# Moving three loads and one weight sum within a fused pooling-attention and MLP kernel

## The chip, the cores and the metric

The kernel runs on one core of a Trainium2 chip. The metric is device time in microseconds from the first to the last instruction of one execution, given as the median of several runs. The engines are TensorE (PE, matmuls; PEld is its weight load), VectorE (DVE), ScalarE (ACT), GpSimd (POOL) and SyncE (SP), which issues most of the data transfers.

## The reference

For each of 8 batches and 8 heads there are 576 positions of width 64. Keys and values are averaged over runs of 8 positions, so that 72 of each are left; queries are not pooled. Attention over the 72 pooled keys is followed by a two-layer perceptron on the joined heads (width 512, hidden width 2048, tanh form of Gelu):

```python
k_p = k.reshape(B, H, 72, 8, D).mean(axis=3)
v_p = v.reshape(B, H, 72, 8, D).mean(axis=3)
attn = softmax(q @ k_p.T / sqrt(D))          # per batch and head
x = (attn @ v_p) laid out as (B*S, 512)      # 4608 rows
out = gelu_tanh(x @ w_in) @ w_out            # (4608, 512), float32
```

## The kernel before

**Groups and steps.** The 4608 rows are worked in nine groups of 512: group b holds positions 0 to 511 of batch b, and one more group (`R`) collects the last 64 positions of all eight batches. `seq` is their order: 0 to 6, R, 7. One step of the program is the perceptron of one group, with the attention of the next group and the loads of the one after that placed between its matmuls. So in step 1 the matmuls are those of group 1, the attention is that of group 2 (`n`), and the loads are for group 3 (`n2`).

**What sets the order.** There is no scheduler: the order on each engine is the order in which the code emits instructions. `at(hooks, s, f, ...)` puts a call at position s of the step. Positions 0 to 63 are the matmuls of the first layer (the hidden half; one per matmul of 512 columns, four matmuls for one of 16 blocks of the hidden layer), and 64 to 175 are those of the second layer (the output half), seven products of 16 matmuls each. Both layers of the later steps use a seven-product scheme in place of eight products, which needs sums of operand blocks: `w_sums` makes four sums of blocks of `w_out` (once, into `tw`), `g_sums` sums of the hidden activations (each step), `x_sums` sums of the inputs. Step 1 uses the plain first layer (`hidden_two`, `hidden`, L554 and L397) and the seven-product second layer; from step 2 on `hidden_fast` does the first layer with seven products too, partly (L500).

**Attention of the next group.** Pooling is three adds on DVE: L162 (8 to 4), L164 (4 to 2), L165 (2 to 1, into `kvb`). For K, `dup_k` (L178) writes a second copy, a DMA transpose (L225, `kTd`) turns it, and GpSimd spreads it into `kbd` (L94). Queries are cast to bf16 (`q_b`, L94 or L92) and turned by a DMA transpose (L246, `qT`). V goes through GpSimd's masked spread (L185, `vbd`). The scores (L262) go to `e` by an exponential on ACT (L271), DVE makes the row sums (`den`, L278) and the reciprocal `r` (L287), POOL or DVE normalises into `eb` (L293), four DMA transposes (L320) give `eT`, and the weighted sums (L358) give `xT`, the next group's input.

**Loads.** K and V of a group lie in the tiles `k_sb` and `v_sb`, each with one buffer; `k_sb` holds 512 of the 576 pooled rows of K in four chunks, and its fifth chunk is half K and half V. So `load_kv` has a K part of three transfers (`k_sb`: 1 MB, 128 KB, 128 KB; part 0) and a V part of one (`v_sb`, 1 MB; part 1). A part can go out only when the pooling of the group before has read the buffer. Queries (`q_sb`, 1 MB, two buffers) are loaded by `load_q` on SP, or by `load_q_behind` on POOL: a one-column copy into `gate` that reads the tile named, and so waits for its landing, and then the transfer from POOL's queue.

**What the change touches.** In step 1 (`n_ == 1`, L861 to L865 and L917 to L939): the place of the third sum of `w_out` blocks, L862; the place and queue of group 3's queries, L919 and L926 to L930; the place of group 3's K part, L938. In step 2 (`n_ == 2`): the first pooling add of group 3's K, L895. In the hidden half of a fast step (L518 to L543), DVE's instructions L525, L533, L536 and L540 free or finish the PSUM banks that PE's products share, and the K pooling stands between them at the position that L895 gives.

Of the kernel before, what the change touches and what calls it, by code (L numbers as in the profile page):

```python
# [19 lines left out]
def kernel(  # L20
# [21 lines left out]
    nc = tc.nc  # L42
    B, H, S, D = q.shape
# [44 lines left out]
    st = [dict() for _ in range(B + 1)]  # L88
# [711 lines left out]
    def at(hooks, s, f, *a):  # L800
        hooks.setdefault(s, []).append(lambda: f(*a))
# [6 lines left out]
    hooks = {}  # L808
# [47 lines left out]
    for n_, g in enumerate(seq):  # L856
        if n_ == 0:
            continue
        hooks = {}
        fast = n_ >= 2  # L860
        if n_ == 1:  # L861
            for i, s in enumerate((1, 10, 14)):  # L862
                at(hooks, s, w_sums, 1 + i, 0, NP, nc.vector)
            at(hooks, 36, g_sums, 0, 4)
            at(hooks, 57, g_sums, 4, 6, (0,))  # L865
        else:
            at(hooks, 41, g_sums, 0, 2, (0,))
            at(hooks, 57, g_sums, 2, 6, (0,))
            at(hooks, 65, g_sums, 6, 8, (0,))
            at(hooks, 65, g_sums, 0, 4, (1,))  # L870
        if not fast:
            at(hooks, 65, g_sums, 6, 8, (0,))
        at(hooks, 64 + 32, g_sums, 4, 8, (1,))
        if n_ == 6:
            at(hooks, 30, late_stores)
        if n_ + 1 < len(seq):
            n = seq[n_ + 1]
            b = B - 1 if n == R else n
            kv = n != B - 1
            if n_ == 1:  # L880
                at(hooks, 18, cast_q, n, 0, 1, nc.scalar)
                at(hooks, 18, cast_q, n, 2, 4, nc.gpsimd)
                at(hooks, 22, cast_q, n, 1, 2, nc.scalar)
                at(hooks, 24, qT_tile, n)
                at(hooks, 24, q_transpose_dma, n)
            if kv and not fast:
                at(hooks, 2, pool, b, 0, 5)
                at(hooks, 2, dup_k, b, 0, 5)
                at(hooks, 2, kT_tile, b, None)
                at(hooks, 2, k_transpose_dma, b)  # L890
                at(hooks, 24, pool, b, 5, 9)
                at(hooks, 26, k_spread, b, [nc.gpsimd, nc.gpsimd])
                at(hooks, 26, spread_v, b, nc.gpsimd)
            elif kv:
                at(hooks, 5, pool, b, 0, 5, (0,))  # L895
                at(hooks, 17, pool, b, 0, 5, (1,))
                at(hooks, 17, dup_k, b, 0, 5)
                at(hooks, 17, kT_tile, b, None)
                at(hooks, 17, k_transpose_dma, b)
                at(hooks, 17, spread_gated, b)  # L900
                at(hooks, 40, k_spread, b, [nc.gpsimd, nc.gpsimd])
            sc_at = [68, 68, 90, 90]
            for j in range(4):
                at(hooks, sc_at[j], scores, n, j)
                at(hooks, sc_at[j] + 1, exps, n, j)
            at(hooks, 80, eT_tile, n)
            for j in range(4):
                at(hooks, 80 if j < 2 else 92, norm, n, j, nc.vector if j > 1 and fast else nc.gpsimd)
                at(hooks, 80 if j < 2 else 92, e_transpose_dma, n, j)
            at(hooks, 64 + 66, nc.scalar.preload_act_table_set, GELU_SET)  # L910
            at(hooks, 64 + 100, xT_tile, n)
            if n_ == 1:
                at(hooks, 64 + 100, values, n, (0,))
                at(hooks, 64 + 107, values, n, (1,))
            else:
                at(hooks, 64 + 104, values, n)
        if n_ + 2 < len(seq):  # L917
            n2 = seq[n_ + 2]
            s2 = 1 if n_ == 1 else 30  # L919
            for half, ahead in enumerate((3, 2)):  # L920
                if n_ + ahead < len(seq) and seq[n_ + ahead] == R:
                    if half == 0:
                        at(hooks, 2, q_tile, R)
                    at(hooks, 2, load_q_behind, R, st[g]["xT"][64:128, KO - 1, MAIN - 1:MAIN], 2 * half, 2 * half + 2)
            if n2 != R:
                at(hooks, s2, q_tile, n2)  # L926
                if n_ == 1:
                    at(hooks, s2, load_q_behind, n2, st[n]["k"][64:128, 4, 7, D - 1:D], 0, 4)
                else:
                    at(hooks, s2, load_q, n2, 0, 4, nc.sync)  # L930
            at(hooks, 64 + 52, cast_gated, n2)
            at(hooks, 64 + 94, qT_tile, n2)
            at(hooks, 64 + 94, q_transpose_dma, n2)
            if n2 != B - 1:
                b2 = B - 1 if n2 == R else n2
                at(hooks, 64 + 84, pool, b2, 5, 9, (0,))
                at(hooks, 64 + 97, pool, b2, 5, 9, (1,))
            at(hooks, 29 if n_ == 1 else 28, load_kv, n2, (0,))  # L938
            at(hooks, 28 if n_ == 1 else 1, load_kv, n2, (1,))  # L939
        mlp(g, hooks, n_ + 1 == len(seq), fast)  # L940

# [29 lines left out]
```

The softmax here doesn't subtract the row's maximum and nothing guards it: scores larger than these inputs give would overflow.

## Time and profile before

| | |
|---|---|
| Time, median of 3 runs | 281.07 us (278.54 to 282.31) |
| Profiled execution | 278.88 us, span 277.2 us |
| PE busy | 269.3 us, 97% of the span |
| DVE / ACT / POOL busy | 226.2 / 176.4 / 86.7 us |
| Data moved | 54.37 MB, mean 196 GB/s |
| Step 1 | about 51.5 to 81.8 us |
| Step 2 | about 81.8 to 109.4 us |

In the profile a group's line names the code line, the engine, the operation, and the output and input tiles; a wait line reads "engine, its line, what it waited for: us in total, times, longest". In the chain and the timelines the first column is the start in us from the start of the span and the second the duration in us. "DMA to landing" is the time from issue of a transfer to its completion.

### The profile page before, as it was taken

The numbers are of one execution on the slowest core, as the hardware profiler recorded it, in microseconds if no ns is written. First come the engines' busy times: TensorE is split into PE (matmuls) and PEld (weight loads), VectorE is DVE, ScalarE is ACT, GpSimd is POOL, SyncE is SP. The second block draws the span as 40 slices with busy tenths as digits, with TensorE's granted clock in tenths as the row PEclk, the third lists the DMA queues.
The fourth block names the chain that finished last, engine by engine and source line by source line (L and its number), as shares of the span: only waits on it lengthen the run. The fifth ranks groups of instructions, "written<-read, shape, count | busy, mean of one in ns | idle before, by whom it ended". The sixth has DMA issues, their size and how long they took to land.

```text
span 277.2 us, 6633 instructions
## 1 busy us (share of the span) xinstructions
PE 269.3 (97%) x2710; PEld 195.5 (71%) x2710; DVE 226.2 (82%) x368; ACT 176.4 (64%) x261; POOL 86.7 (31%) x129
## 2 busy tenths in 40 slices
PE   8989999999999999999999999999999999999995
PEld 3778844445876688668766886688668866886684
DVE  5896869899889899989898999899989458956832
ACT  1576576568546965696469656965696469656820
POOL 4640282045843142224453345233224200300000
PEclk9999999999999999999999999999999999999999
DMA  7999999999989958894999789928393920243013
GB/s 228 310 189 293 368 386 222 281 363 196 266 148 313 283 132 192 257 290 109 193 265 263 193 187 296 234 53 180 118 286 75 173 98 0 50 102 99 2 40 114
DMA packets 67088, 54.37 MB, mean 196 GB/s; under 512 B 41458, under 2 KB 52722, under 8 KB 67058
## 3 DMA queue, kind: packets, MB, share of 16 engines
q1 hardware_dynamic: 64146, 49.62, 68.5%
q0 software_dynamic: 2768, 4.20, 7.7%
q8 instruction: 21, 0.34, 0.5%
q10 hardware_dynamic: 144, 0.13, 0.1%
q14 instruction: 9, 0.07, 0.1%
HBM read 36.70 MB, written 9.44 MB: 166 GB/s over the span
## 4 chain that ended last, share of the span: by engine, by line
PE 65%; DMA 10%; DVE 7%; issue 1%; ACT 1%; POOL 1%; SPq 1%; DVEq 0%; ACTq 0%; POOLq 0%
PE mm L609 28%; PE mm L397 16%; PE c L500 14%; DMA eT<-eb 5%; PE x L609 3%; DMA qT<-q_b 2%; PE xo L358 2%; DMA k_sb<-in_v_dram 2%; PE sc L262 2%; DVE den L278 1%; DVE eb L293 1%; DVE k_sb L162 1%; DVE k_sb L164 1%; DVE kvb L178 0%; ACT e L271 0%
## 5 line engine op out<-in xcount | busy, mean ns | idle before, releaser
L397 PE MATMUL mm<-xT,w_in_b 128*128 128x512 bf16 x280 | 65.5, 379 | 0.4 <-ACT gT L399 0.4
L609 PEld LDWEIGHTS <-gT 128*128 128x128 bf16 x512 | 48.3, 98 | 9.0 <-issue 1.4
L399 ACT ACTIVATE gT<-mm 128x512 bf16<-128x512 f32 x70 | 39.7, 598 | 16.0 <-PE mm L397 15.9
L397 PEld LDWEIGHTS <-w_in_b 128*128 128x128 bf16 x280 | 27.4, 98 | 27.8 <-issue 0.9
L609 PEld LDWEIGHTS <-stage 128*128 128x128 bf16 x384 | 37.6, 98 | 4.3
L293 POOL TENSOR_TENSOR eb<-e,r 128x576 bf16<-128x576 f32 x16 | 18.5, 1179 | 49.2 <-DVE r L287 26.8
L92 ACT CAST xT<-xo 128x512 bf16<-128x512 f32 (+1 forms) x24 | 13.2, 610 | 28.4 <-PE xo L358 24.1
L609 PE MATMUL mm<-tw,gT 128*128 128x256 bf16 x240 | 30.0, 273 | 0.0
L609 PE MATMUL mm<-w_out_b,gT 128*128 128x256 bf16 x240 | 29.9, 273 | 0.0
L271 ACT ACTIVATE e<-sc 128x576 f32<-128x576 f32 x36 | 22.3, 649 | 9.7 <-POOL eb L293 5.4
L278 DVE TENSOR_REDUCE den<-e 128x8 f32<-128x576 f32 x36 | 26.3, 731 | 2.5 <-ACT e L271 2.5
L500 PEld LDWEIGHTS <-ws 128*128 128x128 bf16 x224 | 21.9, 98 | 7.0
L609 PE MATMUL mm<-tw,stage 128*128 128x256 bf16 x224 | 26.7, 273 | 0.0
L92 ACT COPY osb<-mm 128x512 f32<-128x512 f32 x29 | 17.2, 592 | 13.7 <-PE mm L609 13.6
L185 POOL TENSOR_TENSOR vbd<-kvb,vmask 128x256 bf16<-128x256 bf16 (+2 forms) x38 | 21.6, 590 | 5.8 <-DVE kvb L165 4.7
L94 POOL CAST q_b<-q_sb 128x1024 bf16<-128x1024 f32 (+1 forms) x16 | 17.1, 1087 | 19.4 <-DMA q_sb<-in_q_dram 19.4
L500 PE MATMUL c<-tt,ws 128*128 128x256 bf16 x168 | 20.6, 273 | 0.0
L500 PEld LDWEIGHTS <-w_in_b 128*128 128x128 bf16 x168 | 16.4, 98 | 2.4 <-issue 0.2
L408 PE MATMUL mm<-xT,w_in_b 128*128 128x256 bf16 x128 | 15.6, 273 | 0.1
L293 DVE TENSOR_TENSOR eb<-e,r 128x576 bf16<-128x576 f32 x16 | 15.0, 940 | 0.6
L609 PE MATMUL mm<-w_out_b,stage 128*128 128x256 bf16 x128 | 15.3, 273 | 0.0
L459 DVE TENSOR_TENSOR gT<-gT 128x512 bf16<-128x512 bf16 (+1 forms) x24 | 12.9, 536 | 2.4 <-ACT gT L516 0.5
(118 smaller groups left out, 439.1 us busy)
## 6 DMA issues: line engine op xcount, KB each, us to landing
q_sb<-in_q_dram SPq DMA_DIRECT2D x6, 1024.0 KB, 8.8
k_sb<-in_k_dram SPq DMA_DIRECT2D x6, 1024.0 KB, 7.7
v_sb<-in_v_dram SPq DMA_DIRECT2D x6, 1024.0 KB, 8.2
out_dram<-osb SPq DMA_DIRECT2D x12, 512.0 KB, 4.1
w_in_b<-in_moe_w_in_dram POOLq DMA_DIRECT2D x4, 512.0 KB, 6.7
w_out_s<-in_moe_w_out_dram SPq DMA_DIRECT2D x2, 1024.0 KB, 13.9
stage<-in_moe_w_out_dram SPq DMA_DIRECT2D x2, 1024.0 KB, 15.3
out_dram<-osb SPq DMA_DIRECT2D x7, 256.0 KB, 2.8
```

What stands on the lines that cost most here:

```text
L92: eng.copy(out=out, in_=in_)
L94: eng.tensor_copy(out=out, in_=in_)
L185: eng.tensor_tensor(out=vbd[p0:128, b, n0:n1, :].rearrange("p (c r) (hh d) -> p c (r hh) d", c=max(m, 1), d=D), in0=kvb[p0:128, 4 + c0:4 + ...
L271: nc.scalar.activation(out=e.rearrange("p (x h) s -> p x (h s)", x=2), in_=sc[:, :, 0:4 * Sp], func=ACT.Exp, scale=1.0 / 64.0)
L278: nc.vector.reduce_sum(out=den, in_=e, axis=AX.X)
L293: eng.tensor_tensor(out=o.rearrange("p (pr hh s) -> p hh pr s", hh=2, s=Sp), in0=e.rearrange("p (hh pr) s -> p hh pr s", hh=2), in1=r.rear ...
L397: nc.tensor.matmul(out=hp, lhsT=w_in_b[:, ko, fo * 128:(fo + 1) * 128], rhs=st[g]["xT"][:, ko, :], start=(i == 0), stop=(i == KO - 1))
L399: nc.scalar.activation(out=gT[:, fo, :], in_=hp, func=ACT.Gelu_apprx_tanh)
L408: nc.tensor.matmul(out=hp[:, f, :], lhsT=w_in_b[:, ko, (fo + f) * 128:(fo + f + 1) * 128], rhs=st[g]["xT"][:, ko, c0:c0 + 256], start=(i = ...
L459: nc.vector.tensor_tensor(out=a21, in0=a21, in1=a22, op=ALU.add)
L500: nc.tensor.matmul(out=acc[:, m, :], lhsT=lhs(i, m), rhs=rhs(i), start=bool(fresh and i == 0 and m % 2 == 0), stop=(i == 1), skip_group_ch ...
L609: nc.tensor.matmul(out=xs[p] if acc is xs else acc[:, p, :], lhsT=lt, rhs=rt, start=bool(fresh and m == 0 and (p == 0 or (last and acc is ...
```

## The change

Four edits. The third of step 1's `w_sums` moves from hook 14 to hook 97, right behind the sum of `g_sums` that the sixth product reads; what it makes (`tw[3]`) is first read by the seventh product, from hook 160. Group 3's queries go out on SP at hook 29, behind its V part at hook 28, and not on POOL behind the landing of group 2's K tile. Group 3's K part goes from hook 29 to hook 93, which is behind the last two DMA transposes of group 2's softmax weights (hook 92). As K comes later, its first pooling add in step 2 moves from hook 5 to hook 11. The purpose is to keep the loads of group 3 out of the way of group 2's transfers and transposes, and to take the weight sum out of DVE's way ahead of the softmax.

```diff
         if n_ == 1:
-            for i, s in enumerate((1, 10, 14)):
+            for i, s in enumerate((1, 10, 64 + 33)):
                 at(hooks, s, w_sums, 1 + i, 0, NP, nc.vector)
...
             elif kv:
-                at(hooks, 5, pool, b, 0, 5, (0,))
+                at(hooks, 11 if n_ == 2 else 5, pool, b, 0, 5, (0,))
                 at(hooks, 17, pool, b, 0, 5, (1,))
...
-            s2 = 1 if n_ == 1 else 30
+            s2 = 29 if n_ == 1 else 30
...
             if n2 != R:
                 at(hooks, s2, q_tile, n2)
-                if n_ == 1:
-                    at(hooks, s2, load_q_behind, n2, st[n]["k"][64:128, 4, 7, D - 1:D], 0, 4)
-                else:
-                    at(hooks, s2, load_q, n2, 0, 4, nc.sync)
+                at(hooks, s2, load_q, n2, 0, 4, nc.sync)
...
-            at(hooks, 29 if n_ == 1 else 28, load_kv, n2, (0,))
+            at(hooks, 93 if n_ == 1 else 28, load_kv, n2, (0,))
             at(hooks, 28 if n_ == 1 else 1, load_kv, n2, (1,))
```

## The prediction, made before the result was known

> **What bounds the kernel now.** I read the page first, then busy time by stretch, the waits of the tensor engine alone, the chain, and the vector engine's timeline around the edit.
>
> ```profile
> PE 269.3 (97%) x2710; PEld 195.5 (71%) x2710; DVE 226.2 (82%) x368; ACT 176.4 (64%) x261; POOL 86.7 (31%) x129
> ```
>
> PE is the bound: 269.3 of 277.2 us. All that any edit of order can give back is PE's idle time, 7.9 us in the whole span. The stretches show where it lies around the edit (step 1's hidden half, its output half, step 2's hidden half, its output half; after the stretch come length, then busy us of PE, PEld, DVE, ACT, POOL, then clock, DMA share, GB/s):
>
> ```profile
> 53.00:66.00 13.00, 12.60 (x59) 5.57 (x58) 11.44 (x14) 9.29 (x17) 3.92 (x4) 1.00 1.12 289
> 66.00:82.00 16.00, 15.22 (x212) 12.17 (x211) 13.79 (x24) 8.98 (x14) 12.09 (x13) 1.00 1.01 216
> 82.00:95.00 13.00, 13.00 (x90) 8.61 (x88) 11.82 (x18) 10.21 (x15) 3.63 (x8) 1.00 1.04 295
> 95.00:109.00 14.00, 14.00 (x206) 11.72 (x205) 13.24 (x23) 8.05 (x12) 4.80 (x5) 1.00 0.68 153
> ```
>
> Step 1 idles PE 0.40 + 0.78 us; step 2 not at all. So the edit can win at most about 1.2 us where it works, and step 2, which it also touches, can only lose. The waits of PE from 53 to 82 us, and the chain there, name the idle time:
>
> ```profile
> PE sc L262 <- DMA qT<-q_b: 0.6, 1, 0.6
> PE mm L397 <- ACT gT L399: 0.4, 1, 0.4
> ```
>
> ```profile
> 60.39 6.78 DMA qT<-q_b
> 67.17 0.04 issue
> 67.21 0.46 PE sc L262 x32
> ...
> 73.88 4.86 DMA eT<-eb
> 78.75 0.14 issue
> 78.88 0.75 PE xo L358 x16
> ```
>
> The scores of group 2 wait 0.64 us for the query transpose, which takes 6.78 us from issue to landing, where the one of group 3 took 4.4 at 79.60. The weighted sum waits 0.14 us for the second transpose of softmax weights: 4.86 us, where such transposes took 2.6 us in quiet stretches. Both transposes run beside loads of group 3: its queries (GpSimd's queue, issued 56.40, 7.1 us to landing) and its V and K (SyncE's, from 65.12). The 0.40 us is ScalarE: its casts wait for group 2's queries, landed at 57.76, and a Gelu stands behind them.
>
> The vector engine, start and duration:
>
> ```profile
> 60.03 1.21 DVE L451 TENSOR_TENSOR tw<-w_out_b,tw 128x2048 bf16<-128x2048 bf16 x1
> ...
> 70.34 0.74 DVE L278 TENSOR_REDUCE den<-e 128x8 f32<-128x576 f32 x1
> ...
> 82.67 1.49 DVE L162 TENSOR_TENSOR k_sb<-k_sb 128x1280 f32<-128x1280 f32 x1
> 84.07 1.22 DVE L525 TENSOR_TENSOR other<-c,other 128x1024 f32<-128x1024 f32 x1
> ...
> 87.43 1.21 DVE L533 COPY stage<-c 128x1024 f32<-128x1024 f32 x1
> 88.89 1.23 DVE L536 TENSOR_TENSOR stage<-c,stage 128x1024 f32<-128x1024 f32 x1 [0.26 <-PE c L500]
> ```
>
> The first weights became ready at 68.68 (ScalarE's exponentials start at 68.08) but were reduced only at 70.34: DVE was late there by 1.66 us. In step 2 the first half of K's pooling (L162) fills a hole before L525, and everything up to L536 is back to back.
>
> **What the Trainium skill says.** "DMA: Bandwidth & Descriptors", section "Issuing engines are not separate DMA queues": DMAs from GpSimd and SyncE end on the same 16 engines and interleave. The trace agrees: the transposes were slowest (6.4 and 6.8 us) while the GpSimd queue's 1 MB was in flight. The same page, "Measured (HBM→SBUF, 128 partitions, SWDGE, issued from GpSimd)", gives 6.15 us for 1 MB alone; this trace has 5.7 to 10.3 us for the pieces of a K load, and I use those. "SBUF — State Buffer", section "Who interferes with whom": a VectorE instruction with two SBUF inputs and a GpSimd one that reads SBUF lock each other out. The trace agrees: L462 took 0.80 us at 65.72, 1.07 us at 74.29 beside GpSimd's normalisation, one of which took 1.60 us instead of 1.15.
>
> **The change part by part.**
>
> *Third weight sum (1.21 us) from hook 14 to hook 97.* On DVE it leaves 60.03 and comes after the fourth operand sum (L462), at about 74.4. Everything between moves up by at most 1.2 us. The pooling of V(2) right behind it needs V(2)'s landing, 49.55 + 10.8 = 60.35, so I take 1.0. den starts at 69.3, GpSimd's four normalisations (71.44 to 76.37) end near 75.4, and the last weights' transpose, issued at 77.2 now, goes at about 75.5. Behind the sum stand L623 and L594; L594 reads x before the last product may add to it. Now L594 ends at 77.36, 0.78 us before that product (78.14). Then it ends at 77.36 - 1.0 + 1.2 = 77.6 if the sum costs its plain 1.2, and the product is due at 78.14 - 0.64 = 77.5: a stall of 0.1 us, up to 0.5 if the port lock stretches the sum to 1.6. With DVE's 0.70 us idle before L594 to absorb a part, I take 0. V(3)'s pooling and the xT cast behind have 0.69 us of idle time now: 0.
>
> *Queries of group 3 to SyncE at hook 29.* The load leaves GpSimd (a 1.50 us gate and a 0.96 us issue in 55 to 57.4, both inside its wait for group 2's queries: 0). With it gone from 57 to 63 us, group 2's K transpose should take 4.4 us instead of 6.4, its query transpose 4.4 to 5.9 instead of 6.78: landing at 64.8 to 66.3, before PE asks at 66.57. Gain 0.64 us. V(3) and queries then go out behind it at about 62.5 to 63.5 and land by 72 or so, just before the weights' transposes. The 0.40 us stays, since group 2's queries land before the removed load has moved much.
>
> *K of group 3 (1.25 MB) from 65.75 to behind the last weights' transpose.* The weights' transposes lose a competitor (K(3) landed only at 77.1): gain 0.14 us. In its new place K is issued from 76.7, the last of its three pieces at about 77.9. Landing is bounded by 5.7 us (the K load at 116.81) and 10.3 (the K load at 65.75): 83.6 to 88.2. I take the 6.9 of the load at 88.79: 84.8. Queued behind it on SyncE are group 3's query transpose (needed only near 95), two stores and V(4): 1.7 us of issue, no one waits: 0.
>
> *Its pooling from hook 5 to hook 11 of step 2.* On DVE L162 now stands behind L525 and two L482. L525 can start when ScalarE's copy ends, 82.75 + 1.01 = 83.8 (all on the old clock). Then 83.80 + 1.13 + 0.34 + 0.33 = 85.6 for L162, + 1.5 + 0.85 + 0.53 + 0.2 = 88.7 for L533, where it was 87.43: 1.28 us later, because the hole of 1.1 us that L162 filled stays empty. L533 then ends at 89.92 and the product that needs its bank (89.66) waits 0.3; L536 ends at 91.18, and the product due at 90.53 + 0.3 waits 0.4 more. Cost 0.7 us. It is less (0.1) if the matmuls have slack that I don't see, more by whatever K is late: on the old clock K is wanted at 85.6, which after a gain of 0.8 is 84.8. That is exactly where I put the landing; each us later costs a us, since PE has then no slack left. K(3)'s transpose shifts to about 88.7, lands by 93.1, and its spread still ends before the scores near 95: 0.
>
> *Sum.* -0.64 - 0.14 + 0.7 + about 0 for lateness = -0.1 us: 281.0.
>
> **The rivals.**
> *Faster:* step 2 hides the later pooling, and the 0.8 us of step 1 stays, perhaps with the 0.4 us as well: 279.9 to 280.3. For it: DVE waits in step 2 now (0.26 and 0.46 us before L536 and L540). Against it: the empty hole is longer than these waits.
> *Slower:* the load is late. Its neighbours are the last transposes (they issue slowly, up to 1.84 us each), the query transpose and 1 MB of stores from 81.4. With 9 to 10 us to landing K arrives at 87 to 88, PE waits 2 to 3 us more behind L533: -0.8 + 0.7 + 2.5 = +2.4, 283.5. For it: the 1.2 us of earliness on DVE may not reach the transposes, which sat in a queue. Against it: two later K loads took 5.7 to 7.1.
>
> **How the numbers follow.** About even 0.5, faster 0.25, slower 0.25. Three runs of the kernel before lie from 278.54 to 282.31, wider than most of these cases differ. From the sum, 280.3 less 1.9 for a low draw and 281 to 283.5 on the other side: 278.4 to 283.1. Faster by over 2% would need 275.4 us: 5.6 us from some 1.2 us of idle time, 0.02. Slower by over 2% needs K some 5 us late: 0.03.
>
> **What would show it.** Right: no wait of the scores for the query transpose near 66 us; den at about 69.3; V(3) and queries on SyncE near 63, K(3) near 77; L525 ahead of L162 in step 2, L533 about 1.3 us later against PE, PE idle 0.5 to 1 us in step 2's hidden half. Wrong: DVE idle before L162 for over 1 us (K late), a wait of the last product for L594, the query transpose still over 6 us (then not the GpSimd queue's load but V(2) or K slowed it), or a shift in steps 3 to 8, which should keep their 27.5 us each.

## The result, and the profile after

The changed kernel takes 281.61 us (median of 21 runs, 279.77 to 283.02) where the kernel before takes 279.64 (21 runs beside them, 278.54 to 283.08). The ratio is 1.0056, 95% interval 1.0033 to 1.0078: slower by about 1.6 us. Ratios, here and below, leave out the few executions that ran slow as a whole, and need not equal the ratio of the medians beside them. The forecast was 281.0 us and no change. That 281.61 is so near to it is luck: the forecast started from the median of three runs, 281.07, and 21 runs of the same kernel have 279.64. Counted from there, it missed a loss of 1.6 us.

The profiled execution spans 280.3 us, 3.1 more than that of the kernel before. The two differ by more than the medians do: the kernel before was profiled in an execution near the fast end of its times, 278.88 us. Busy time by stretch, columns as in the prediction:

```profile
53.00:66.00 13.00, 12.34 (x57) 5.47 (x56) 10.06 (x12) 9.12 (x17) 6.62 (x7) 1.00 1.06 233
66.00:82.00 16.00, 15.53 (x213) 12.27 (x212) 15.16 (x25) 9.17 (x15) 9.43 (x9) 1.00 0.74 212
82.00:95.00 13.00, 12.39 (x85) 8.02 (x84) 11.35 (x17) 9.40 (x13) 2.95 (x7) 1.00 1.09 284
95.00:109.00 14.00, 14.00 (x196) 11.44 (x198) 13.31 (x23) 8.11 (x12) 5.93 (x7) 1.00 0.76 201
```

Step 1 idles PE 0.66 + 0.47 us where it was 0.40 + 0.78, so nothing is won there: PE's first product of step 2 starts at 81.68 us in both traces. Step 2's hidden half, where PE had no idle time, now has 0.61 us. PE's own timeline gives the waits (start, duration, instruction, and in brackets the idle time before it and what ended it):

```profile
59.22 7.21 PE L397 MATMUL mm<-xT,w_in_b 128*128 128x512 bf16 x32 [0.66 <-ACT gT L399]
...
78.36 0.60 PE L609 MATMUL mm<-tw,gT 128*128 128x256 bf16 x4 [0.47 <-DVE osb L594]
...
89.95 1.03 PE L500 MATMUL c<-xT,ws 128*128 128x256 bf16 x8 [0.29 <-DVE stage L533]
91.31 1.03 PE L500 MATMUL c<-tt,w_in_b 128*128 128x256 bf16 x8 [0.33 <-DVE stage L536]
...
136.57 0.97 PE L358 MATMUL xo<-eT,vbd 32*64 32x256 bf16 x24 [0.39 <-DMA eT<-eb]
153.04 0.22 PE L262 MATMUL sc<-kbd,qT 64*64 64x72 bf16 x2 [0.96 <-POOL kbd L94]
153.60 0.45 PE L262 MATMUL sc<-kbd,qT 64*64 64x72 bf16 x30 [0.35 <-POOL kbd L94]
181.95 0.45 PE L262 MATMUL sc<-kbd,qT 64*64 64x72 bf16 x30 [0.58 <-POOL kbd L94]
```

The wait of the scores for the query transpose at 67 us is gone, and so is that of the weighted sum at 78.75. In their place stand L594 in step 1, L533 and L536 in step 2, a wait of the weighted sums for `eT` in step 3, and waits of the scores for `kbd` in steps 4 and 5. Starts tell more than the idle time, since the ends of matmuls are modelled. In the chain, the last block of step 2's hidden half starts at 91.41 us in the kernel before,

```profile
91.41 3.45 PE mm L397 x16
```

and at 92.35 us in the changed kernel:

```profile
92.35 3.45 PE mm L397 x16
```

Both steps began together, so step 2 lost 0.94 us.

The vector engine around the edit:

```profile
74.95 2.17 DVE L451 TENSOR_TENSOR tw<-w_out_b,tw 128x2048 bf16<-128x2048 bf16 x1
77.03 0.68 DVE L623 TENSOR_TENSOR osb<-mm,osb 128x512 f32<-128x512 f32 x1
77.64 0.67 DVE L594 TENSOR_TENSOR osb<-mm,osb 128x512 f32<-128x512 f32 x1
...
83.80 1.23 DVE L525 TENSOR_TENSOR other<-c,other 128x1024 f32<-128x1024 f32 x1 [0.56 <-ACT other L523]
...
85.61 1.49 DVE L162 TENSOR_TENSOR k_sb<-k_sb 128x1280 f32<-128x1280 f32 x1
...
88.69 1.21 DVE L533 COPY stage<-c 128x1024 f32<-128x1024 f32 x1
90.03 1.23 DVE L536 TENSOR_TENSOR stage<-c,stage 128x1024 f32<-128x1024 f32 x1
```

The moved weight sum (L451) takes 2.17 us instead of 1.21. L162 stands behind L525 and does not wait for K: the bracket for a wait is missing, and K's last piece, issued at 78.69 us, landed 6.1 us later, at 84.8. SyncE's queue, of the kernel before:

```profile
79.60 1.73 SPq L246 DMA_TRANSPOSE qT<-q_b  x1
81.42 1.58 SPq L439 DMA_DIRECT2D out_dram<-osb  x2
83.09 1.17 SPq L125 DMA_DIRECT2D v_sb<-in_v_dram  x1
87.54 1.20 SPq L225 DMA_TRANSPOSE kTd<-kvb  x1
```

and of the changed kernel:

```profile
77.52 0.57 SPq L125 DMA_DIRECT2D k_sb<-in_k_dram  x1
78.13 0.51 SPq L120 DMA_DIRECT2D k_sb<-in_k_dram  x1
78.69 0.59 SPq L118 DMA_DIRECT2D k_sb<-in_v_dram  x1
79.40 5.04 SPq L246 DMA_TRANSPOSE qT<-q_b  x1
84.53 0.99 SPq L439 DMA_DIRECT2D out_dram<-osb  x2
85.62 0.88 SPq L125 DMA_DIRECT2D v_sb<-in_v_dram  x1
88.80 1.20 SPq L225 DMA_TRANSPOSE kTd<-kvb  x1
```

The query transpose behind K holds SyncE for 5.04 us instead of 1.73. The stores and V of group 4 go out 2.5 to 3.1 us later. V was under way in the kernel before too when the K transpose of group 3 was issued, but it landed at 91.3 us, and now at 94.1. The transpose, issued 1.3 us later because of the later pooling, lands behind V in both: at 92.0 us and at 94.7. From issue to landing, V and then the transpose took in the kernel before

```profile
DMA to landing us min/median/max: 8.2/8.2/8.2
```

```profile
DMA to landing us min/median/max: 4.4/4.4/4.4
```

and in the changed kernel

```profile
DMA to landing us min/median/max: 8.5/8.5/8.5
```

```profile
DMA to landing us min/median/max: 5.9/5.9/5.9
```

### The profile page after: what moved, and what is told of

It is laid out like the page before. It is cut to its first block, busy times and chain, and to the rows that moved or that the text cites. A ratio compares the mean times of both kernels' runs of the same rounds, so it can differ in the third digit from the quotient of the medians.

```text
span 280.3 us, 6632 instructions
## 1 busy us (share of the span) xinstructions
PE 269.7 (96%) x2710; PEld 194.8 (70%) x2710; DVE 226.1 (81%) x368; ACT 176.4 (63%) x261; POOL 86.9 (31%) x127
## 4 chain that ended last, share of the span: by engine, by line
PE 61%; DMA 10%; DVE 10%; POOL 2%; ACT 2%; issue 1%; SPq 1%; DVEq 0%; ACTq 0%; POOLq 0%
PE mm L609 28%; PE mm L397 14%; PE c L500 11%; DMA kTd<-kvb 5%; DMA q_sb<-in_q_dram 3%; PE x L609 2%; PE xo L358 2%; PE sc L262 2%; DMA eT<-eb 1%; DVE den L278 1%; DVE other L525 1%; DVE eb L293 1%; POOL kbd L94 1%; ACT e L271 1%; DVE k_sb L164 1%
## 5 line engine op out<-in xcount | busy, mean ns | idle before, releaser
L185 POOL TENSOR_TENSOR vbd<-kvb,vmask 128x256 bf16<-128x256 bf16 (+2 forms) x38 | 22.6, 616 | 5.8 <-DVE kvb L165 4.7
L458 DVE TENSOR_TENSOR stage<-gT 128x512 bf16<-128x512 bf16 (+1 forms) x24 | 13.0, 543 | 2.8 <-ACT gT L516 2.8
L516 ACT ACTIVATE gT<-other 128x1024 bf16<-128x1024 f32 x14 | 14.8, 1055 | 0.0
```

The source lines that it names most:

```text
L185: eng.tensor_tensor(out=vbd[p0:128, b, n0:n1, :].rearrange("p (c r) (hh d) -> p c (r hh) d", c=max(m, 1), d=D), in0=kvb[p0:128, 4 + c0:4 + ...
L516: nc.scalar.activation(out=gq[:, MQ:MQ + 4, e, c:c + 256], in_=src, func=ACT.Gelu_apprx_tanh)
```

## The experiments

The letters change their meaning on the way. In the first four runs, theory A says that two placements on DVE carry the loss, the weight sum beside GpSimd's normalisation and K's pooling behind L525; rival B says that it is the late K's load or landing, with DVE's order free. In the next four, theory A says that the late K carries the loss, because its pooling behind L525 leaves a hole on DVE empty and makes L533 and L536 late, and because the late load delays V(4), which is ahead of the K transpose; rival B says, in the first two of them, that the weight sum beside GpSimd's work carries about half of it. In the last three, theory C says that V ahead of the K transpose takes the slack of the scores, and rival D that the slow landings come from elsewhere. All ratios are to the kernel before, on the same chip.

**The weight sum alone.**

```diff
-            for i, s in enumerate((1, 10, 14)):
+            for i, s in enumerate((1, 10, 64 + 33)):
```

> Kernel before with one edit: the third weight sum at hook 97. Theory A (two placements on DVE carry the loss: the weight sum beside GpSimd's normalisation, and K's pooling behind L525): the sum takes about 2 us instead of 1.2, L594 is late and the last product of step 1 waits up to 0.5 us for it; but den starts earlier, so the net is 0 to +0.5 us (ratio 1.000 to 1.002). Rival B (the loss comes from the late K load alone, DVE's order costs nothing): no wait for L594, ratio 0.998 to 1.000.

Ratio 1.0002 (0.9978 to 1.0026). On DVE the sum was as long as in the changed kernel:

```profile
73.95 2.17 DVE L451 TENSOR_TENSOR tw<-w_out_b,tw 128x2048 bf16<-128x2048 bf16 x1
```

den came 1.3 us earlier (69.00), as the prediction had it. L594 ended at 77.3 us, before the last product came at 77.6, so there was no wait: PE was itself 0.42 us late from the query transpose, and DVE a us earlier than in the changed kernel, since V(2) landed at 59.9 us here and at 60.7 there. The long sum is as theory A had it, the missing wait as the rival had it, and the interval holds both; a cost or a gain of the sum alone is not to be told from zero. In steps 3 and 4 this trace shows the waits for `eT` and `kbd` of the changed kernel too (0.40, and 0.96 + 0.35 us), with K loaded early; those waits are no mark of the whole change.

**The pooling alone.** K is loaded early and only pooled later.

```diff
-                at(hooks, 5, pool, b, 0, 5, (0,))
+                at(hooks, 11 if n_ == 2 else 5, pool, b, 0, 5, (0,))
```

> Kernel before with one edit: K's first pooling add of step 2 at hook 11, the K load where it was. Theory A: L533 starts about 1.25 us later against PE, PE waits some 0.3 + 0.4 us for L533 and L536 in step 2, +0.7 to +1.0 us in all (ratio 1.002 to 1.004), with K long landed. Rival B: the waits of step 2 came from K's landing, so here there are none and the ratio is 1.000.

Ratio 1.0030 (1.0006 to 1.0054), 0.8 us. PE in step 2:

```profile
90.23 1.03 PE L500 MATMUL c<-xT,ws 128*128 128x256 bf16 x8 [0.29 <-DVE stage L533]
91.59 1.03 PE L500 MATMUL c<-tt,w_in_b 128*128 128x256 bf16 x8 [0.33 <-DVE stage L536]
```

These are the changed kernel's two waits to 0.01 us, with K long in its place. So they come from DVE's order, not from the landing; the rival of this run is out. This trace, of one of the longest executions of the run (282.62 us), also has the changed kernel's waits for `eT` (0.61 us) and for `kbd` in steps 4 and 5 (1.31 and 0.58 us), though K comes early.

**The queries alone.**

```diff
-            s2 = 1 if n_ == 1 else 30
+            s2 = 29 if n_ == 1 else 30
...
-                if n_ == 1:
-                    at(hooks, s2, load_q_behind, n2, st[n]["k"][64:128, 4, 7, D - 1:D], 0, 4)
-                else:
-                    at(hooks, s2, load_q, n2, 0, 4, nc.sync)
+                at(hooks, s2, load_q, n2, 0, 4, nc.sync)
```

> Kernel before with one edit: queries of group 3 on SyncE at hook 29, ahead of its K part; the weight sum, K's load and pooling as before. Theory A: kTd of group 2 lands in 3 to 4.5 us instead of 6.4, the scores' wait of 0.64 us goes, but 1 MB more is in flight at 72 us, so the weights' transposes are slower than 4.9 us and the weighted sum waits 0.3 to 1 us: -0.6 to +0.4 us (ratio 0.998 to 1.001). Rival B: the K load so close to V and queries is what hurts, +1 us or more (ratio over 1.003).

Ratio 1.0003 (0.9973 to 1.0033), in theory A's range. The K transpose of group 2 landed in 3.0 us instead of 6.4 and the query transpose in 5.2 instead of 6.8; the scores did not wait. But V, queries and K then came in one block, K landed 10.2 to 10.5 us after issue, and the gain was paid back a few us later:

```profile
78.05 0.75 PE L358 MATMUL xo<-eT,vbd 32*64 32x256 bf16 x16 [0.64 <-DMA eT<-eb]
```

**The queries, and the second weight sum in a hole of DVE.** The queries' edit as above, and

```diff
-            for i, s in enumerate((1, 10, 14)):
+            for i, s in enumerate((1, 1, 14)):
```

> As the run with the queries alone, and the second weight sum at hook 1 instead of 10, where DVE sat idle 1.1 us before group 2's K landed. Theory A: den of group 2 starts some 1 us earlier without a sum beside GpSimd, so GpSimd's normalisations and the weights' transposes are earlier and nothing is paid in step 2: -0.8 to 0 us (ratio 0.997 to 1.000), 0.3 us or more below the run with the queries alone. Rival B: the same as the run with the queries alone.

Ratio 0.9994 (0.9967 to 1.0022). den came at 69.84 against 69.67 with the queries alone, in a trace that runs 0.6 us later from 50 us on: 0.4 us earlier and not 1, since DVE then waits 0.29 us for V(2) to land. The weighted sum waited 1.22 us for the weights' transposes. The expected gain over the queries alone, 0.3 us or more, is not shown: the intervals are wider than that.

**All but the late K.** The changed kernel with K's part back at hook 29 and its pooling at hook 5.

```diff
-                at(hooks, 11 if n_ == 2 else 5, pool, b, 0, 5, (0,))
+                at(hooks, 5, pool, b, 0, 5, (0,))
...
-            at(hooks, 93 if n_ == 1 else 28, load_kv, n2, (0,))
+            at(hooks, 29 if n_ == 1 else 28, load_kv, n2, (0,))
```

> The changed kernel with K's part of the load back at hook 29 and its pooling back at hook 5; the weight sum at hook 97 and the queries on SyncE stay. Theory A (the loss is the late K: its pooling behind L525 costs 0.8 us, and the delayed V(4) takes the slack of step 2's scores): no waits for L533 or L536, kTd of group 3 lands in under 5 us, time as before, ratio 0.997 to 1.002. Rival B (the weight sum beside GpSimd and the crowded queue carry about half of the loss): ratio 1.002 to 1.004.

Ratio 1.0015 (0.9993 to 1.0037). No wait in step 2, and the K transpose of group 3 landed in 3.8 us. In step 1 the last product waited for L594:

```profile
77.80 0.60 PE L609 MATMUL mm<-tw,gT 128*128 128x256 bf16 x4 [0.52 <-DVE osb L594]
```

Theory A's range holds it; the interval also holds a part of rival B. Here too the scores of steps 4 and 5 waited for `kbd`, 0.98 us in each, with K loaded early.

**The changed kernel without the sum's move.**

```diff
-            for i, s in enumerate((1, 10, 64 + 33)):
+            for i, s in enumerate((1, 10, 14)):
```

> The changed kernel with the third weight sum back at hook 14. Theory A: the wait of the last product for L594 (0.47 us) goes, but den and the weights' transposes are later by up to 1 us, and K with them: the late K still costs its whole price, ratio 1.004 to 1.008. Rival B: the sum carries half of the loss, ratio 1.002 to 1.004.

Ratio 1.0034 (1.0010 to 1.0058): in rival B's range, with the interval reaching into A's. Beside the changed kernel's 1.0056, taking back the sum's move wins 0.0022 and taking back the late K (the run above) 0.0041; so the K looks like the larger part. The intervals overlap, and whether the sum costs anything once it meets the rest is not shown. The wait for L594 is gone, the two in step 2 stay (0.28 and 0.33 us). New is what the prediction had costed at nothing: the scores of step 2 wait for `kbd`, GpSimd's spread of the K transpose, which landed after 6.7 us.

```profile
95.09 1.39 POOL L94 COPY kbd<-kTd 64x288 bf16<-64x288 bf16 x2 [3.77 <-DMA kTd<-kvb]
```

```profile
96.54 0.45 PE L262 MATMUL sc<-kbd,qT 64*64 64x72 bf16 x30 [0.58 <-POOL kbd L94]
```

**The late K alone**, with its pooling at hook 11, on the kernel before.

```diff
-                at(hooks, 5, pool, b, 0, 5, (0,))
+                at(hooks, 11 if n_ == 2 else 5, pool, b, 0, 5, (0,))
...
-            at(hooks, 29 if n_ == 1 else 28, load_kv, n2, (0,))
+            at(hooks, 93 if n_ == 1 else 28, load_kv, n2, (0,))
```

> Kernel before with K of group 3 at hook 93 and its pooling at hook 11; weight sum and queries as before. Theory A: the waits for L533 and L536 (0.6 to 0.7 us) as with the pooling alone, and on top the stores and V(4) go out some 2 us later on SyncE, so that kTd of group 3 lands in 5 us or more and step 2's scores have under 1 us of slack after kbd: ratio 1.003 to 1.007, above that of the pooling alone (1.003). Rival B: no more than the pooling alone, 1.001 to 1.003.

Ratio 1.0057 (1.0031 to 1.0083): as much as the whole change. Only its times are used here. It is above the pooling alone (1.0030), as theory A has it, but the intervals overlap.

**The changed kernel with the pooling back at hook 5**, so that DVE meets K's landing.

```diff
-                at(hooks, 11 if n_ == 2 else 5, pool, b, 0, 5, (0,))
+                at(hooks, 5, pool, b, 0, 5, (0,))
```

> The changed kernel with K's pooling back at hook 5 while K still comes at hook 93. Theory A: DVE sits before L162 from about 82.8 us to K's landing near 85.1, with L525 behind it, and L533 comes about 1 us later than in the changed kernel: ratio 1.007 to 1.012. Rival B (hook 11 was the mistake, K would have been there in time): DVE does not wait, ratio 1.001 to 1.004.

Ratio 1.0043 (1.0017 to 1.0068): a loss, but not the larger one that theory A expected (1.007 to 1.012). The rival, that K would have been in time, fails in its mechanism: DVE waits for K, and PE behind it for L525:

```profile
84.65 1.49 DVE L162 TENSOR_TENSOR k_sb<-k_sb 128x1280 f32<-128x1280 f32 x1 [1.36 <-DMA k_sb<-in_v_dram]
```

```profile
87.33 1.03 PE L500 MATMUL c<-tt,ws 128*128 128x256 bf16 x8 [1.09 <-DVE other L525]
```

L533 came at 89.42, 0.73 us later than in the changed kernel. So with K late, both places cost; what hook 11 saves here is not resolved in the times.

**V behind the K transpose.** What was left to explain were the waits for `kbd`. In steps 2 to 5, V of the next load goes out at hook 1, ahead of the K transpose at hook 17. This run takes it out of the way, on the kernel before:

```diff
-            at(hooks, 28 if n_ == 1 else 1, load_kv, n2, (1,))
+            at(hooks, 28 if n_ == 1 else 20, load_kv, n2, (1,))
```

> Kernel before with one edit: in the steps from 2 on, the V part of the next loads goes out at hook 20, behind the K transpose (hook 17), and not at hook 1 ahead of it. Theory C (the steps' scores have little slack because 1 MB of V stands ahead of the K transpose on the DMA engines; in executions where V lands slowly the scores wait for kbd): kTd lands in under 4 us in every step, kbd ends 2 us or more before the scores, and the upper half of the times comes down: -0.5 to -1.2 us (ratio 0.996 to 0.998). Rival D (the slow executions come from elsewhere, kTd is slow for itself): kTd as before, ratio 1.000; or V lands too late for its pooling and the time rises by 1 us or more.

Ratio 0.9986 (0.9966 to 1.0006), 279.64 us: a gain is not shown, for the interval holds both theory C's range and no change. But the upper end of the times came down, as theory C had it: the 22 executions lie between 278.62 and 280.63 us, where 13 of the 48 of the kernel before lie above 280.63, up to 281.81. The K transposes (six issues; some traces lack one landing) took, in the kernel before, the changed kernel and this run:

```profile
DMA to landing us min/median/max: 2.6/5.1/6.4
```

```profile
DMA to landing us min/median/max: 2.6/5.9/7.6
```

```profile
DMA to landing us min/median/max: 2.6/2.6/6.5
```

The 6.5 is that of step 1, which the edit does not touch. In step 4 `kbd` now ends 3.6 us before the scores ask for it; in the kernel before GpSimd was done at 150.8 us, as the scores began:

```profile
147.66 0.91 POOL L94 COPY kbd<-kTd 64x288 bf16<-64x288 bf16 x2
```

```profile
152.21 0.45 PE L262 MATMUL sc<-kbd,qT 64*64 64x72 bf16 x32
```

**The changed kernel with V behind the K transpose** (the same one-line edit).

> The changed kernel with the same edit of V. Theory A with C: the waits for L533 and L536 in step 2 (0.6 us) and for L594 (0.5 us) stay, but kbd of group 3 ends over 1.5 us before the scores, and so in the steps behind it: 1.0 us or so below the changed kernel, ratio to the kernel before 1.000 to 1.003. Rival D: 1.005 to 1.006 as the changed kernel.

Ratio 1.0004 (0.9976 to 1.0032), 280.22 us. Its interval lies just below the changed kernel's (1.0033 to 1.0078). With this edit in both, the change still costs 0.6 us by the medians, 279.64 and 280.22. The waits that DVE's order makes are still there, and from step 1 on no scores wait:

```profile
78.02 0.60 PE L609 MATMUL mm<-tw,gT 128*128 128x256 bf16 x4 [0.55 <-DVE osb L594]
89.61 1.03 PE L500 MATMUL c<-xT,ws 128*128 128x256 bf16 x8 [0.29 <-DVE stage L533]
90.97 1.03 PE L500 MATMUL c<-tt,w_in_b 128*128 128x256 bf16 x8 [0.32 <-DVE stage L536]
```

**The queries on SyncE with V behind the K transpose**, both on the kernel before.

> Kernel before with the queries of group 3 on SyncE at hook 29 and V behind the K transpose from step 2 on. Theory C: no waits in step 2, the scores of step 1 do not wait (0.64 us), the weighted sums of step 1 wait up to 1.2 us for the weights' transposes; -0.5 to -1.3 us, ratio 0.995 to 0.999. Rival D: ratio 1.000 as with the queries alone.

Ratio 0.9981 (0.9956 to 1.0006), 279.51 us, the lowest median of all runs. No scores wait from step 1 on, and the weighted sums of step 1 wait 0.85 us, as theory C had it; but that it beats the kernel before is not shown, for the interval holds 1.

## Why the prediction was wrong, point by point

**The bound** was read rightly: PE gave and took all of it, and nothing came near 2%.

**The step 1 gain of 0.78 us** came to nothing, and the step that failed is "I take 0" for the wait of the last product for L594. The mechanism of the gain held: both named waits are gone, the K transpose landed in 3.1 us (4.4 forecast), the query transpose in 5.6 (4.4 to 5.9 forecast). Two terms took it back. The wait for L594, with 0.5 as the far end in the prediction, was 0.47 us, because the sum took 2.17 us; with 1.2 us L594 would have ended near 77.3, before the product was due at 77.89. The prediction allowed for up to 1.6 us, and counted on DVE's idle time before L594 and on an earlier den; with V(2) landing at 60.7 us, den was only 0.34 us earlier (70.00, 69.3 forecast). The other 0.26 us is ScalarE's wait for group 2's queries, 0.66 instead of 0.40: they landed 0.3 us later. It varies without the change (0 with the sum alone, 0.58 with V moved alone), and is taken for chance.

**The later pooling, 0.7 us**, was right in mechanism and low in size. L533 was forecast at 88.7 and came at 88.69; L536 was forecast to end at 91.18 and ended at 91.26. PE's two waits, 0.29 and 0.33 us, are the 0.3 and 0.4 of the forecast; by the starts of PE's blocks the cost was 0.94 us, and where the other 0.3 lie is not read from the trace. The run with the pooling alone has the same two waits: ratio 1.0030, about 0.8 us, of which its waits in later steps may be a part.

**K's landing** was forecast for 84.8 us, came at 84.8, and was wanted at 85.6. In part that is luck: the last piece went out 0.8 us later than forecast and took 0.8 us less. The rival "the load is late" did not happen.

**"Queued behind it on SyncE ... no one waits: 0" and "its spread still ends before the scores near 95: 0"** are the other steps that failed. The prediction added 1.7 us of issue to SyncE; but the query transpose, now queued behind 1.25 MB, held SyncE for 5.04 us instead of 1.73, and V(4), and the K transpose behind it, landed 2.7 to 2.8 us later. That took all of the slack of the chain through GpSimd, which the prediction had left out of the sum. In the kernel before GpSimd was done at 93.0 us and the scores began at 95.2. In the changed kernel GpSimd's spread ended at 96.19 us, and the scores of step 2 began at 96.17:

```profile
94.74 1.45 POOL L94 COPY kbd<-kTd 64x288 bf16<-64x288 bf16 x2 [2.99 <-DMA kTd<-kvb]
```

```profile
96.17 0.53 PE L262 MATMUL sc<-kbd,qT 64*64 64x72 bf16 x32
```

In this execution it was just in time; in the run without the sum's move it was 0.58 us too late. The cause can be read in the landings: in step 2 V(4) and the K transpose landed at 91.3 and 92.0 us in the kernel before, at 94.1 and 94.7 in the changed one, at 90.0 and 90.7 in the run of the sum alone, at 94.4 and 95.1 in the one without the sum's move: in all four the transpose lands 0.6 to 0.7 us after V. Taking V out of the way, in steps 2 to 5 at once, brought the changed kernel from 1.0056 to 1.0004.

**"Steps 3 to 8 should keep their 27.5 us each"** did not hold in the profiled execution: steps 4 and 5 waited 1.31 and 0.58 us for `kbd`. V and the K transpose took 11.8 and 7.6 us in step 4, against 8.9 and 5.7 before, with SyncE's queue at the same places relative to the step. The run of the sum alone shows the same (11.9 and 7.8), the one of the queries alone does not (8.1 and 5.3). So it comes and goes between executions. In these two steps V is not alone ahead of the K transpose: the queries of `R`, four pieces from GpSimd's queue, go out with it, and the transpose lands 0.6 us after the last of them all (V at 151.7 and the queries at 151.6 us in step 4, queries at 179.5 in step 5). Moving V behind the transpose also brought these queries in sooner, the last of them 5.4 us after its issue in step 4 instead of 10.6. No run moves the queries of `R` alone, so in steps 4 and 5 V is not shown to be the one to blame.

**The sum**, then: about 0 in step 1 instead of -0.78, and +0.94 in step 2 instead of +0.7. The rest of the 1.6 us, some 0.7 by subtraction, is put down to waits for `kbd`, forecast at 0. The two traces cannot be used to size it: they differ by 2.2 us from step 3 on, and traces of runs with K early have such waits too. The evidence is the changed kernel with V moved, whose loss beside the same edit of the kernel before is 0.6 us; so about 1 us of the 1.6 goes with V's place. What stays open is whether the change makes slow landings in steps 4 and 5 more frequent, or whether the later V(4) in step 2 alone makes the difference: one trace per kernel does not tell, and the intervals of the runs with the late K overlap.

## What to carry to other kernels

When a load is moved behind other work on a queue, cost what is queued behind it by when it lands, not by the time to issue it: the next copy in the queue may end up in front of a transpose on which another engine has little slack. Where an engine works back to back for a stretch, a hole that an operation fills is worth about what the hole is long; moving that operation later costs the hole again (here 0.94 us for a hole of 1.1), whatever the move wins elsewhere. And in a kernel whose matmul engine is 97% busy, look first for the latest-starting short chain to it (here pooling, transpose, spread, scores) and clear its path.

## What the runs showed of the hardware that was not expected

A VectorE sum of two 128x2048 bf16 operands in SBUF took 2.17 us beside GpSimd's normalisation in the five traces that have it there (changed kernel, sum alone, all but the late K, pooling back at 5, changed kernel with V moved), and 1.20 to 1.23 us where GpSimd was idle; another of these sums took 2.02 to 2.06 us where a GpSimd cast had started before it, in five traces (pooling alone, queries alone, all but the late K, without the sum's move, queries with V moved). That is up to nearly double, where the lock that the Trainium skill describes ("SBUF — State Buffer", section "Who interferes with whom") was priced at 0.4 us from a trace of the kernel before. It can go the other way: in the changed kernel a sum and a GpSimd cast started together at 58.1 us; the sum kept its 1.21 us, and the cast took 2.10 us where it took 1.03 in the kernel before.

A K transpose of 128x640 bf16 (160 KB) landed 2.6 us after its issue, or 0.4 to 0.8 us after the last load issued ahead of it, whichever was later; so it was from step 2 on in every trace but that of the late K alone, with up to 7.8 us from issue to landing. The issue of a query transpose (512 KB) held SyncE for 4.6 to 5.0 us behind the 1.25 MB of K in four of these traces, for 4.2 to 4.7 us in step 1 of the four in which 1 MB from GpSimd's queue was under way, and for 1.5 to 3.6 us elsewhere. The same 1 MB load of V in step 4 took 8.1 to 9.1 us in four traces and 11.0 to 11.9 in five, at the same place of the program; why is not known.
